# VectorE waits for each GpSimd power before its next two-input instruction, under re-searched engine orders

## The chip, the cores and the metric

The kernel runs on one core of a Trainium2 chip. The metric is the device time of one execution in microseconds (us); the figure for a kernel is the median of several runs. A core has five engines that work side by side, each through its own queue in order: TensorE (matrix products, PE in the profile), VectorE (DVE), ScalarE (ACT), GpSimd (POOL) and SyncE (SP, which here only issues transfers). They wait for one another through semaphores.

## The reference

Two blocks follow each other on a sequence of 2048 rows and 640 columns, in bf16.

```python
def layernorm(x):                        # over the 640 columns, eps 1e-5
    return (x - mean(x)) / sqrt(var(x) + eps)

def A(q, k, v):                          # a gated long convolution
    k_shift = sum(k shifted down by t rows * shift_k[:, t] for t in range(4))
    kv = k_shift * v
    y = irfft(rfft(pad(kv)) * rfft(pad(ssm_k)))[:2048]   # causal, along the rows
    return q * (y + kv * ssm_D)

h = x + A(layernorm(x), A_k, A_v)        # x is A_q
g = silu(layernorm(h) @ w_gate)          # 640 -> 1728
u = layernorm(h) @ w_up
out = h + (g * u) @ w_down               # 1728 -> 640
```

## The kernel before

The 2048 rows are cut into four blocks of 512 (j = 0 to 3), and the columns of the convolution into two halves of 320 (c = 0, 1). For each block and half the kernel works in stages:

- VectorE forms kv: four products of shifted rows of k with the taps, added up, times v. In blocks 2 and 3 two of the additions are made by accumulating transfers that GpSimd issues (line 1089, `kvd`).
- TensorE transforms blocks of kv and of the filter to frequencies with tables (line 694 is the one place where nearly all matmuls are recorded); ScalarE and VectorE copy the results out of PSUM (lines 677, 678, 680, 681). Between two steps of the transform SP's queue shuffles rows by transfers (`sh`, `rs`; line 685). Block 0 uses dense tables and no shuffles.
- VectorE multiplies spectra of pairs of blocks (`m1`, `m2`), adds (`ac`) and combines them (`cr`, `ci`); all these are tensor-by-tensor instructions recorded at line 913.
- TensorE transforms back; VectorE multiplies with the normed q and adds x, which gives h.
- The second layer norm is formed from statistics of h (lines 1003, 1007), h is normed (`hn`), turned (line 1223, or by a transfer for blocks 2 and 3), and the feed-forward runs on it: per block 27 groups of five matmuls with 512 columns, then the product with w_down. ScalarE computes silu (line 1249), VectorE the product of g and u.

The feed-forward of a block is put beside the convolution of later blocks, so that TensorE has work while spectra are formed.

Each layer norm has a short chain of tiny instructions on 2 or 4 columns: VectorE forms variance plus eps (line 1018, `va`; a negated mean at 1045 or 1058), **GpSimd raises it to the power -0.5** (line 1019, `nr`), and VectorE multiplies the negated mean with the result (line 1021, `nm`). The norms themselves (lines 1028 on VectorE, 1029 on ScalarE) use both. There are 12 such powers: one for each block's first norm (4 columns), two for each block's second (2 columns each).

The order on each engine is neither that of the code nor chosen on the chip. All 1640 operations are listed first; a planner (`schedule`) then plays the program through with a duration for each operation and transfer, and at every moment gives a free engine the ready operation with the lowest rank. The ranks are the table `_ORDER`; where an operation could go to ScalarE or VectorE, the table `_WHO` may fix it ("a" or "d"), or the planner chooses. The sequence that comes out is emitted, with semaphores where operations depend on each other; the planner's times themselves are not enforced.

The planner knows that [...] operations of VectorE [...] are marked `lock` (products, combinations, kv, norms, `nm`), and while a power is planned on GpSimd it starts none of them:

```python
if e == "pool" and o.dma is None and c > 0.5 and free["dve"] > t + 1e-9 and dvelock:
    continue
if e == "dve" and o.lock and (poolend > t + 1e-9 or waits):
    continue
```

`deps` of an operation holds the operations that it depends on, with a kind (2: it needs their results); `emit` turns each into a wait.

Of the kernel before, what the change touches and what calls it, by code (L numbers as in the profile page):

```python
# [16 lines left out]
794 795 796 414 566 793 416 567 1244 1246 1235 600 601 1245 198 258 259 857 791 790 401 23 204 24 260 429 785 427 423 199 797 425 433 110 207 421 205  # L17
244 111 0 59 54 71 62 4 19 45 77 69 79 150 101 81 83 93 60 161 163 413 5 120 118 145 82 80 125 50 42 76 91 100 18 20 17 159 151 47 128 555 301 563 147
157 149 1239 10 13 379 377 153 1242 178 181 155 48 1249 102 282 419 43 399 409 11 74 78 44 66 170 84 70 9 206 63 380 146 126 119 117 109 483 99 431 49
248 381 245 190 378 197 270 179 127 67 172 187 995 913 665 660 376 349 672 98 65 893 915 905 890 909 372 675 663 849 272 875 505 865 867 991 979 327  # L20
637 983 336 628 515 647 869 292 559 499 575 855 551 871 985 517 583 316 827 31 507 297 495 287 661 561 981 821 645 716 553 286 466 977 513 873 340 649
639 7 92 1322 158 808 934 710 1001 141 148 90 1090 1410 706 144 75 73 446 448 162 169 171 160 152 108 273 89 34 33 30 36 256 544 949 1314 27 744 736
189 180 107 186 432 177 116 464 291 538 540 748 477 407 405 411 403 221 266 156 154 579 463 535 418 757 1347 533 233 1455 428 1437 484 398 40 953 277
531 246 406 400 243 404 420 470 537 467 306 276 1296 1308 1286 442 482 452 756 438 1011 1274 424 402 412 479 557 581 835 829 195 386 545 541 473 1226
542 532 997 255 168 536 222 462 465 534 478 441 475 408 268 1217 451 1304 711 907 367 530 685 422 426 731 430 1069 1071 345 802 1029 951 1003 232 410
55 15 1221 1447 1433 1445 552 554 779 769 1359 1431 1349 504 497 6 25 383 550 715 443 453 1209 730 471 279 543 219 275 1414 578 1021 695 690 705 961
1223 1065 1048 1031 1063 696 191 1298 959 686 1023 134 56 37 700 72 88 1212 142 95 139 86 390 96 138 801 1200 1105 691 539 112 113 165 1067 1049 1045
1204 137 1230 94 1284 1232 889 184 132 185 183 87 135 46 106 701 1203 1425 188 1372 1192 122 175 176 807 1061 803 1324 58 57 1222 1316 1092 1408 1406
1107 1601 1109 1117 1326 1346 958 1318 1348 1089 1412 1093 1416 1420 721 1418 391 1201 1208 1184 726 32 741 1144 1369 105 1073 1046 1427 1435 1214
1218 1227 35 1177 236 1160 238 254 1589 1302 749 1104 1598 573 1199 385 447 281 449 384 1439 1429 39 38 241 265 1210 237 1597 1635 1152 1590 299 1593  # L30
735 274 681 1594 933 1231 677 395 51 1075 725 1573 1550 1565 1553 1557 1566 1009 1282 936 358 1280 1276 917 1007 1005 396 1577 1019 1017 525 1278 911
892 1581 1582 523 167 53 166 174 524 164 196 1225 1344 1375 264 1549 1631 740 290 1025 417 247 445 218 227 1569 262 1632 1633 1606 1605 1604 1619 1637
1586 415 919 720 240 999 1574 1558 250 269 267 1636 450 1626 1617 1288 501 440 789 472 1 1027 363 480 234 476 474 1585 444 788 1120 1126 194 1030 220
41 782 784 1376 1143 1561 1554 1442 932 935 308 1127 253 242 488 457 239 772 754 547 607 520 1334 257 1111 783 508 588 436 437 261 510 511 577 589 289
16 251 263 252 298 435 792 548 1616 284 1623 1129 68 1329 560 556 834 439 956 210 212 209 203 202 1492 1190 762 1335 1135 1125 1113 64 8 519 136 828
1356 1095 1423 1094 224 910 493 460 973 1510 817 455 387 487 486 459 456 458 1252 974 21 213 352 781 434 1255 1154 635 26 344 115 397 229 114 522 1494
1336 1328 343 226 1331 1436 1333 1136 461 812 481 1262 1467 1464 1147 1198 201 528 1119 215 1610 490 836 454 571 492 1176 658 216 235 231 230 217 225
278 1123 1599 1466 1450 1465 498 502 586 516 514 131 1629 813 1193 503 1026 1366 1350 738 967 1517 1536 1518 1525 1503 133 61 1013 1630 489 491 603
1578 1562 1628 1627 1471 1139 1620 1167 1175 1156 1453 644 833 831 1506 1150 1050 1271 670 1166 1502 1012 249 839 512 1474 1378 1470 1480 1488 966 280
562 1591 1462 1365 359 1155 1486 1535 1402 1399 1370 1128 1137 1377 1482 1243 1367 1342 494 1362 1368 1361 1615 1614 1195 1461 1456 1237 1512 1514  # L40
1138 1267 1454 1478 1339 814 1258 1256 1380 569 633 1458 1490 1392 1178 1430 1452 837 1241 1261 818 1388 939 938 856 1238 228 1179 1130 758 285 496
1300 140 529 124 208 970 1294 1545 1608 776 1338 1440 780 1358 1432 1352 1360 1131 1354 1141 1263 1140 1533 816 392 143 1162 283 1142 763 1133 1132
1310 1424 994 564 1463 565 634 393 1153 895 500 587 103 786 1260 806 1158 805 859 1014 931 1270 388 1428 1364 1363 733 1311 1583 1403 810 394 97 1043
632 1247 368 85 1382 1215 1422 568 1253 1404 708 52 1250 1248 558 271 1259 1174 468 469 546 22 1371 1374 993 12 549 1609 858 767 753 1499 1236 3 838
1257 1341 1254 1373 1146 1186 1438 1426 771 14 1080 1460 787 1390 214 485 1306 1309 1612 1216 1234 1475 745 350 930 940 2 1596 1103 1530 798 799 927
945 900 929 928 104 1290 1240 1015 1625 894 1264 1496 570 925 923 28 1613 1383 1497 1495 1493 1543 1624 1618 593 303 1041 1042 1522 1484 1052 992 1038
1516 313 1476 1587 1559 1602 293 1546 29 323 580 173 572 318 692 625 1555 357 619 627 123 590 1018 947 1016 1024 950 960 1151 304 687 602 830 1417 819
1110 1570 954 1086 1639 1051 952 1057 1055 1054 902 683 1397 1084 804 682 1079 1039 924 922 920 926 121 832 1020 962 1028 1022 679 182 712 693 826
1498 295 1085 506 702 314 1393 1622 707 1081 1082 1066 1058 732 1078 697 1272 1500 722 576 574 1056 1087 1621 1207 1059 1077 678 618 636 1547 1391 509
518 822 1441 809 703 1444 1097 646 868 1033 1528 1224 1443 1485 1389 1487 389 1459 1229 717 1379 1548 1537 1538 288 305 1053 1037 1035 582 584 689 294  # L50
1083 300 1407 713 1508 684 611 1386 1384 727 846 840 1098 1076 1451 1449 597 1387 1072 1062 1068 1064 1515 638 1187 1477 1394 1395 1396 904 347 596
815 626 309 1096 614 1161 594 880 610 604 1595 820 1398 737 310 1099 612 914 1197 874 1060 1044 1047 1457 864 872 862 860 521 606 616 1145 842 1483
1544 863 851 1564 1196 1381 1580 1191 1163 1385 1468 608 1171 824 1202 1206 1600 1603 1002 1275 1074 1233 1285 1542 1185 1194 1446 1448 1183 1088 1526
1159 1323 1507 848 1532 1529 980 976 688 629 854 324 1114 1115 320 642 328 972 338 968 643 319 694 192 1070 718 774 1415 1405 850 1520 315 723 1579
1551 698 704 699 728 982 870 852 1409 1101 1102 1489 1000 330 988 325 876 333 329 648 844 334 984 365 714 709 659 1172 891 371 1189 811 374 1091 1220
916 742 1330 1540 1472 1531 1534 1504 1479 1188 1413 1469 335 948 729 527 1315 1006 193 1148 1501 664 990 375 978 986 866 346 1434 955 348 1411 906
366 339 719 1419 1401 1513 1511 965 724 651 1320 1481 1523 129 1297 957 1307 1295 1353 1305 674 662 963 1283 1008 1321 1112 364 623 969 1180 1400 1168
1277 734 1181 130 1169 620 1303 1281 353 307 1313 739 1173 1273 1010 996 1004 1279 888 908 912 373 918 370 369 743 342 1287 1157 1164 337 1134 599 595
825 847 609 598 311 617 1165 317 1289 1291 1251 1106 605 1116 773 641 650 881 1491 351 585 764 360 211 1521 1355 1345 1228 355 765 1108 296 1219 613
302 1205 853 761 1301 1124 1149 361 897 901 899 884 640 878 971 666 671 800 680 747 746 998 362 841 654 341 657 655 631 332 331 630 668 652 526 223  # L60
653 987 989 382 200 1319 321 1121 751 676 843 322 861 326 312 1213 1040 941 1118 1036 1034 1332 1357 356 1122 964 1268 946 1269 1032 845 624 944 823
615 937 1343 621 622 592 1312 943 354 760 1299 1293 766 942 755 750 877 1327 1317 1325 759 1340 770 1351 752 1337 778 777 1421 591 1292 1100 667 768
# [44 lines left out]
class Prog:  # L107
# [147 lines left out]
    def schedule(self, bias):  # L255
# [10 lines left out]
        t = 0.0  # L266
        left = len(self.ops)
        while left:
            done_any = True
            while done_any:  # L270
                done_any = False
                for e in ("pe", "dve", "act", "sp", "pool"):
# [60 lines left out]
                    if e == "dve":  # L333
                        dvelock = o.lock
# [1055 lines left out]
```

## Time and profile before

| | us |
|---|---|
| median of 7 runs | 297.61 |
| lowest and highest | 296.79, 300.62 |
| profiled execution, its own time | 297.77 |
| its span, first to last instruction | 296.0 |
| TensorE busy | 282.2 (95%) |
| VectorE busy | 235.7 (80%) |
| ScalarE busy | 200.3 (68%) |
| GpSimd busy | 33.1 (11%) |
| the 12 powers (line 1019) together | 19.2 |

A row of the profile's second part has one digit for each fortieth of the span: the busy share in tenths. The chain of waits follows the execution back from its last instruction: at each step to what released it, or to the instruction before it on its engine. A timeline line gives the start, the duration, the engine and line, what is written and read with its shape and count, and in brackets the idle time before it and what ended that. Where several instructions are merged, the duration runs from the start of the first to the end of the last. A line of the waits gives who waited for whom, the total, the number of times and the longest.

### The profile page before, as it was taken

How to read it: one execution, taken by the hardware profiler on the slowest of the kernel's cores; microseconds unless marked ns; L12 is line 12 of the kernel's file. 1: busy time of each engine (PE TensorE's matmuls, PEld its weight loads, DVE VectorE, ACT ScalarE, POOL GpSimd, SP SyncE). 2: the span in 40 equal slices, each digit the busy share in tenths (PEclk: the TensorE clock that was granted, in tenths of full speed). 3: DMA queues.
4: the chain of work that ended last, by engine and by line, in shares of the span. 5: the costliest groups of instructions: out<-in, count | busy, mean ns of one | idle time of the engine just before them, and what ended most of it. 6: DMA issues, size and time to landing. Idle time of an engine off the chain costs nothing.

```text
span 296.0 us, 5206 instructions
## 1 busy us (share of the span) xinstructions
PE 282.2 (95%) x1820; PEld 153.7 (52%) x1820; DVE 235.7 (80%) x479; ACT 200.3 (68%) x484; POOL 33.1 (11%) x31
## 2 busy tenths in 40 slices
PE   7898979799999899999999999999999999999996
PEld 1465645444444356664445467654444676444574
DVE  3999899998999889999999999992899753214422
ACT  3388889999888878777899895778995221242000
POOL 2000500208111121101100313100020020000000
DMA  6999999835685788728802037754001143000001
GB/s 185 331 368 377 300 359 308 269 121 125 168 179 145 179 200 212 222 67 202 222 33 103 1 91 204 176 132 180 24 0 44 47 90 89 2 0 0 2 22 66
DMA packets 44051, 43.25 MB, mean 146 GB/s; under 512 B 14895, under 2 KB 38889, under 8 KB 43898
## 3 DMA queue, kind: packets, MB, share of 16 engines
q1 hardware_dynamic: 39640, 38.30, 41.6%
q0 software_dynamic: 3328, 3.97, 8.3%
q10 hardware_dynamic: 1058, 0.66, 0.7%
q8 instruction: 14, 0.23, 0.4%
q14 instruction: 11, 0.09, 0.1%
HBM read 20.63 MB, written 2.62 MB: 79 GB/s over the span
## 4 chain that ended last, share of the span: by engine, by line
PE 70%; DVE 12%; ACT 8%; DMA 4%; POOL 3%; issue 2%; ACTq 0%; DVEq 0%; SPq 0%
PE ps L694 69%; DVE sb L913 10%; ACT sb L677 5%; DMA sb<-sb 4%; POOL stt L1019 3%; ACT sb L1029 1%; ACT sb L680 1%; PE ps L823 1%; DVE sb L678 0%; DVE sb L1028 0%; PE ps L1223 0%; DVE sb L779 0%; DVE sb L681 0%; ACT sb L1049 0%; DVE stt L1003 0%
## 5 line engine op out<-in xcount | busy, mean ns | idle before, releaser
L694 PE MATMUL ps<-sb 128*128 128x320 bf16 (+1 forms) x1220 | 227.6, 340 | 6.1 <-DVE sb L913 2.0
L913 DVE TENSOR_TENSOR sb<-sb 128x1280 bf16<-128x1280 bf16 (+3 forms) x286 | 171.1, 658 | 4.2 <-ACT sb L677 3.5
L694 PEld LDWEIGHTS ps<-sb 128*128 128x128 bf16 (+1 forms) x1220 | 116.6, 99 | 100.1 <-issue 7.9
L677 ACT ACTIVATE sb<-ps 128x320 bf16<-128x320 f32 (+2 forms) x282 | 111.4, 483 | 26.2 <-PE ps L694 21.3
L694 PE MATMUL ps<-sb,tab 128*64 128x320 bf16 (+2 forms) x512 | 63.3, 302 | 3.6 <-DMA sb<-sb 2.5
L913 DVE TENSOR_TENSOR sb<-ps,sb 128x512 bf16<-128x512 f32 (+2 forms) x46 | 28.0, 617 | 44.7 <-PE ps L694 38.4
L1249 ACT ACTIVATE sb<-ps 128x512 bf16<-128x512 f32 (+1 forms) x56 | 33.8, 606 | 33.0 <-PE ps L694 32.5
L694 PEld LDWEIGHTS ps<-sb,tab 128*64 128x64 f16 (+2 forms) x512 | 31.6, 101 | 35.7 <-issue 13.3
L1019 POOL TENSOR_TENSOR stt<-stt 128x2 f32<-128x2 f32 (+1 forms) x12 | 19.2, 1601 | 134.6 <-DVE stt L1018 94.8
L1029 ACT ACTIVATE sb<-sb,stt 128x320 bf16<-128x320 bf16 (+1 forms) x31 | 22.3, 750 | 7.0 <-DVE stt L1021 6.6
L680 ACT ACTIVATE sb<-ps 128x320 bf16<-128x320 f32 x49 | 18.5, 447 | 5.1 <-PE ps L694 4.8
L1089 POOL DMA_DIRECT2D sb<-sb x12 | 12.4, 1031 | 68.4 <-DVE sb L913 34.0
L678 DVE CAST sb<-ps 128x320 bf16<-128x320 f32 x26 | 12.0, 481 | 3.4 <-PE ps L694 3.4
L1003 DVE BATCH_NORM_STATS2 stt<-sb 128x6 f32<-128x320 bf16 x32 | 14.4, 477 | 0.0
L1049 ACT ACTIVATE sb<-sb,stt 128x640 bf16<-128x640 bf16 x16 | 13.5, 842 | 0.7 <-DVE stt L1045 0.6
L1042 ACT ACTIVATE sb<-sb 128x640 bf16<-128x640 bf16 x16 | 11.9, 742 | 0.6 <-DMA sb<-in_A_q_dram 0.5
L1028 DVE TENSOR_SCALAR sb<-sb,stt 128x320 bf16<-128x320 bf16 (+1 forms) x17 | 6.2, 383 | 0.7 <-DMA sb<-sb 0.7
L823 PE MATMUL ps<-sb 128*128 128x128 bf16 (+1 forms) x48 | 3.9, 231 | 0.4 <-ACT sb L677 0.3
L823 PEld LDWEIGHTS ps<-sb 128*128 128x128 bf16 (+1 forms) x48 | 3.2, 119 | 1.7 <-issue 1.4
L1223 PE MATMUL ps<-sb 128*128 128x128 bf16 x40 | 3.1, 219 | 0.9 <-ACT sb L677 0.9
L1021 DVE TENSOR_TENSOR stt<-stt 128x2 f32<-128x2 f32 (+1 forms) x12 | 1.8, 146 | 2.4 <-POOL stt L1019 2.4
L681 DVE TENSOR_SCALAR sb<-ps 128x320 bf16<-128x320 f32 x7 | 3.3, 480 | 0.4 <-PE ps L694 0.4
(24 smaller groups left out, 24.3 us busy)
## 6 DMA issues: line engine op xcount, KB each, us to landing
sb<-sb SPq DMA_DIRECT2D x72, 160.0 KB, 2.2
sb<-sb POOLq DMA_DIRECT2D x12, 320.0 KB, 4.2
out_dram<-sb SPq DMA_DIRECT2D x16, 160.0 KB, 2.0
sb<-in_A_k_dram SPq DMA_DIRECT2D x8, 280.0 KB, 3.4
sb<-in_B_w_down_dram SPq DMA_DIRECT2D x13, 160.0 KB, 6.6
sb<-cst_den SPq DMA_DIRECT2D x8, 256.0 KB, 7.4
sb<-in_A_v_dram SPq DMA_DIRECT2D x6, 320.0 KB, 5.3
sb<-in_A_q_dram SPq DMA_DIRECT2D x6, 320.0 KB, 4.6
```

What stands on the lines that cost most here:

```text
L677: fns = {"act": lambda a: a.activation(out=dst(), in_=src(), func=ACTF.Copy), "dve": lambda v: v.tensor_copy(out=dst(), in_=src())}
L678: "dve": lambda v: v.tensor_copy(out=dst(), in_=src())}
L680: fns = {"act": lambda a: a.activation(out=dst(), in_=src(), func=ACTF.Copy, scale=scale), "dve": lambda v: v.tensor_scalar(out=dst(), in0 ...
L694: return lambda t: t.matmul(o(), l(), r(), start=st, stop=sp)
L913: return lambda v: v.tensor_tensor(out=o(), in0=a(), in1=b_(), op=op)
L1003: vec(dve1(CW, False), lambda v: v.bn_stats(st6(l, j, b, c), V(xt, b * D + c * CW, CW)), [(xt, (b, c))], [(ST, ("s", l, j, b, c))], prio, ...
L1019: P.op({"pool": 0.75}, lambda g: g.tensor_tensor(out=y, in0=va, in1=stt[:, 420:420 + hi - lo], op=ALU.pow), c1 + [(ST, "half")], c3, prio, ...
L1029: "act": lambda a: a.activation(out=dst(), in_=src(), func=ACTF.Identity, scale=rs(l, j, b), bias=tmv(l, j, 3)[:, b:b + 1])},
L1042: P.op({"act": act_c(D) + 0.22}, lambda a, b=b, jt=jt: a.activation(out=V(jt, 0, D), in_=V(xt, b * D, D), func=ACTF.Copy, accum_out=tmv(l, ...
L1049: P.op({"act": act_c(D) + 0.3}, lambda a, b=b, jt=jt: a.activation(out=V(jt, 0, D), in_=V(xt, b * D, D), func=ACTF.Square, bias=tmv(l, j, ...
L1089: P.op({"pool": 1.35}, [lambda g: g.dma_start(v4(t0), src(), accum_op=ALU.add)], [(t0, 0)] + cells, [(t0, 0)], prio, dma=(2.1, 2.1, 0.8), ...
L1249: P.op({"act": act_c(n)}, lambda a: a.activation(out=dst(), in_=src(), func=ACTF.Silu), rd, wr, -1000, name=f"si{nm}", after=after)
```

## The change

`schedule` remembers the last power that it has placed on GpSimd. When it next places an operation on VectorE that is marked `lock`, it adds the power to that operation's dependencies, so that `emit` puts a wait for the power ahead of it; then it forgets the power. This is done once for each power, for the first such operation in VectorE's sequence.

The two tables are replaced: all ranks of `_ORDER`, and `_WHO`, where 174 operations in place of 182 are fixed to ScalarE and 58 in place of 52 to VectorE. The search that made the new ranks varied the delays of transfers only. The operations themselves, their number, shapes and buffers stay as they are.

```diff
 _ORDER = """
-794 795 796 414 566 793 416 567 1244 1246 1235 600 601 1245 198 258 259 857 791 790 401 23 204 24 260 429 785 427 423 199 797 425 433 110 207 421 205
...
+797 857 856 794 795 414 1236 1237 547 417 839 566 500 601 569 416 836 567 796 790 791 81 83 20 270 276 467 545 495 297 1142 1444 1443 18 827 1508 1245
...
@@ def schedule(self, bias):
-        pemode, dvelock, poolend = 0, False, 0.0
+        pemode, dvelock, poolend, last = 0, False, 0.0, None
...
                     if e == "dve":
                         dvelock = o.lock
+                        if o.lock and last is not None:
+                            o.deps[last] = 2
+                            last = None
                     if e == "pool" and o.dma is None and o.engs[e] > 0.5:
-                        poolend = t + o.engs[e]
+                        poolend, last = t + o.engs[e], o
```

## The prediction

> **What bounds the kernel now.** I read the page's 40 slices first, then its chain of waits, then the timelines of VectorE and GpSimd around each power.
>
> ```profile
> PE   7898979799999899999999999999999999999996
> DVE  3999899998999889999999999992899753214422
> POOL 2000500208111121101100313100020020000000
> ```
>
> A slice is 7.4 us. TensorE looks busy everywhere, but a busy TensorE need not be at its peak, so I counted its matmuls by form in stretches. Late in the kernel (250 to 270 us) 48 matmuls of 512 columns fill 10 us: 0.208 us each, 0.407 ns per column. At that rate (forms on half the array run in pairs, so they count half) the 97,200 columns of 0 to 60 us are worth 39.6 us: 20.4 us lost. From 60 to 80 us only 1.3 us is lost, from 80 to 110 us 4.6 us, from 110 to 230 us some 0.6 us in ten, and then almost nothing up to 280. So TensorE sets the end from 60 us on, and time can be won in two places: ahead of 60 us, where VectorE and ScalarE feed it (from 20 to 60 us VectorE is idle for 1.7 us of 40, ScalarE for 2.9), and between 80 and 110 us. The chain says the same, with GpSimd on it:
>
> ```profile
> PE 70%; DVE 12%; ACT 8%; DMA 4%; POOL 3%; issue 2%; ACTq 0%; DVEq 0%; SPq 0%
> L1019 POOL TENSOR_TENSOR stt<-stt 128x2 f32<-128x2 f32 (+1 forms) x12 | 19.2, 1601 | 134.6 <-DVE stt L1018 94.8
> ```
>
> L1019 is the power (the reciprocal root of a layer norm), 12 times; 3% of the span is two of them, 3.73 us at 30.7 and 5.20 us at 66.9. Now GpSimd's timeline, and VectorE's beside it:
>
> ```profile
> 30.73 3.72 POOL L1019 TENSOR_TENSOR stt<-stt 128x4 f32<-128x4 f32 x1 [26.34 <-DVE stt L1018]
> 53.45 0.70 POOL L1019 TENSOR_TENSOR stt<-stt 128x2 f32<-128x2 f32 x1 [19.00 <-DVE stt L1058]
> 66.89 5.19 POOL L1019 TENSOR_TENSOR stt<-stt 128x4 f32<-128x4 f32 x1 [11.24 <-DVE stt L1018]
> ```
>
> ```profile
> 30.56 2.99 DVE L913 TENSOR_TENSOR sb<-sb 128x640 bf16<-128x640 bf16 x6
> 34.49 0.16 DVE L1021 TENSOR_TENSOR stt<-stt 128x4 f32<-128x4 f32 x1 [0.94 <-POOL stt L1019]
> ...
> 53.35 0.88 DVE L1003 BATCH_NORM_STATS2 stt<-sb 128x6 f32<-128x320 bf16 x2
> ...
> 66.72 4.50 DVE L913 TENSOR_TENSOR sb<-sb 128x512 bf16<-128x512 bf16 x7
> 72.11 0.16 DVE L1021 TENSOR_TENSOR stt<-stt 128x4 f32<-128x4 f32 x1 [0.90 <-POOL stt L1019]
> ```
>
> The reader is to see that the power at 30.73 ends 0.90 us after the last of six products (30.56 + 2.99 = 33.55; 34.45), the one at 66.89 ends 0.86 us after the last of seven (71.22; 72.08), and that VectorE then stands idle for it anyway. The one at 53.45, beside statistics with a single input, took 0.70. A power alone costs 0.7 to 0.9 us; the rest of a long one is waiting behind products. Five are long (3.72, 5.19, 1.20, 2.27, 1.52): 9.9 us over 0.8 each.
>
> [...] Of a wait on GpSimd the trace has its own number: 0.03 to 0.04 us from a power's end to the start of L1021. [...]
>
> **The change part by part.** It adds a wait: in the planner's order, the first instruction of VectorE marked `lock` after a power depends on that power. Where that instruction is L1021 itself the wait is there already. The planner kept such instructions out of a power's 0.75 us before too, but nothing held the engine to it. No instruction is added or removed; all ranks are new, and of the places by hand ScalarE has 174 for 182, VectorE 58 for 52.
>
> *The wait at 30.7 us.* The power ends by about 31.6 instead of 34.45, and L1021 comes 2.8 us earlier. The six products that stood ahead now stand behind it, about 0.9 us later; the 0.94 us of idling after them goes, so VectorE loses nothing net. ScalarE's norms (L1029, from 34.88) can start up to 2.8 us earlier. But VectorE and ScalarE are all but full here, so most of this is one piece of work before another. What I can point to is TensorE's 1.27 us of idling at 39.67, put down to L1029. Bounds: 0 and 2.8 us of gain; I take 0.9.
>
> *The wait at 66.9 us.* L1021 comes 4.3 us earlier, the seven products 0.9 us later, idle again exchanged (0.90). GpSimd's next instruction, the issue of an accumulating transfer at 72.04, comes earlier as well. TensorE is at 94% of its late rate up to 80 us (filled by the feed-forward), so nothing is won at once. On the chain this power leads through L1028 and ScalarE to a shuffle at 77.40 and to TensorE at 81.87. What may be won is the loss between 80 and 110 us above the usual 0.6 in ten: 4.6 - 1.8 = 2.8 us, of which these waits are part:
>
> ```profile
> 81.87 0.84 PE L694 MATMUL ps<-sb,tab 128*64 128x320 bf16 x8 [0.39 <-DMA sb<-sb]
> 103.97 1.79 PE L694 MATMUL ps<-sb,tab 128*128 128x320 bf16 x12 [1.85 <-DMA sb<-sb]
> ```
>
> The second waits for a shuffle of a later stage, which the new order may or may not start sooner. Bounds 0 and 2.8 us; I take 1.0, about a third.
>
> *The other ten.* Seven took 0.69 to 0.89 and had no one in their way: nothing. The three at 110.77, 163.63 and 215.63 lose 0.4 + 1.5 + 0.7 us; their L1021 didn't wait, and TensorE runs at 92 to 95% of its late rate there: no gain. Each wait can cost VectorE up to 0.9 us, 2.7 in all. Cover: feed-forward matmuls on TensorE, and VectorE's own idle time after 200 us (6.8 us in 200 to 220). I take nothing; without the cover it costs those 2.7.
>
> *The new order.* The 72 shuffles on SP's queue, the 16 smaller ones that spread filter rows, its loads, and the 12 accumulating transfers of GpSimd (1.03 us to issue, 4.2 to land) can move past each other. The profile of before can't show where. Bound it by what transfers cost TensorE directly now, 2.5 us in three waits: 2.5 won if all go, 2.5 lost if as many come. The six more places on VectorE are at most 6 × 0.48 = 2.9 us of it, off ScalarE at 0.46 each. I take nothing and keep ±2.5 for the range.
>
> Sum: 0.9 + 1.0 = 1.9 us. The profiled execution took 297.77 us, 1.77 of it around its span of 296.0; the median of the seven runs is 297.61. So the span falls to about 294.1, and the median to **295.7 us**.
>
> **The rivals.**
> - *Both delays return in full.* 2.8 + 2.8 = 5.6 us, so 292.0. For it: both powers are on the chain. Against: VectorE is idle for only 1.7 us between 20 and 60 us, 0.9 of which is exchanged.
> - *Hidden anyway.* Before 60 us work fills VectorE and ScalarE whatever its sequence; after it TensorE is full. Then the time stays at 297.6. The table of busy engines speaks for this; the 1.27 and 1.85 us of idling TensorE against.
> - *Slower: VectorE stands for a power that is late itself.* GpSimd takes its queue in order, and its accumulating transfers wait for one another there:
>
> ```profile
> POOL sb L1089 <- DMA sb<-sb: 11.2, 3, 4.1
> ```
>
> Three waits, the longest 4.1 us. A power that comes behind such an issue is late by up to 4.1 + 0.9 for the issue; before, VectorE ran on with products, now all its instructions behind the first product stand, with them the inverse transforms on TensorE and the ScalarE copies after them. Price 4.1 + 0.9 = 5.0 us a time. VectorE is idle for 6.3 us in all between 10 and 200 us, so one such stall with the 2.7 us above is more than it can take back (7.7 over 6.3), and at the front nothing covers it. One stall uncovered, less the 1.9 won: 300.7 us. Against: five powers (109.9 to 186.1 us) stand between accumulating transfers now, and each was released by VectorE, none by a transfer. A new order that hardware follows worse ends on this side too.
> - *The change doesn't do what it says*: if the search has put L1021 or single-input work after each power, the added waits are empty and the new order alone acts. A short power then still shows that the order did it; the gain is the same.
>
> **How the numbers follow.** A measurement here tells about 0.5% (1.5 us) from no change: 296.1 and 299.1. The forecast, partial return (294.0 to 296.5), gets 0.38, of which 0.02 lies within 0.5%; full return 0.13; hidden 0.19; slower 0.30, large because an order that wins on paper has no profile yet. Faster 0.36 + 0.13 = 0.49, same 0.02 + 0.19 = 0.21, slower 0.30. Range 292.8 to 300.7: it leaves out half of full return and some four tenths of the slower cases. The likeliest case alone: 294.0 to 296.5.
>
> **What would show it.** Right: no power over 1.0 us (L1019 about 9.5 us in all for 19.2); POOL at 1% or less on the chain; waits of L913 or another product for L1019, under 1 us each; first feed-forward matmul ahead of 60.6 us; fewer than 4.6 us lost from 80 to 110 us. Wrong: a wait for L1019 of several us on VectorE; powers short but feed-forward no earlier (hidden); TensorE idle after 110 us.

## The result, and the profile after

The change made the kernel slower: 301.44 us median of 12 runs (299.56 to 303.78) against 297.92 for the kernel before in the same comparison; the ratio is 1.0112, with a 95% interval of 1.0083 to 1.0142. A second comparison gave 1.0100 (1.0072 to 1.0129). The forecast was 295.7, the range ended at 300.7. Medians are of all executions; ratios and their intervals leave out a few slower ones (over 1.5% above the fastest), so the two need not agree to the last digit.

The profiled execution took 299.56 us, the shortest of its twelve, with a span of 297.8. All lines of the code stand three further down: the power is L1022, the product with its result L1024, VectorE's tensor-by-tensor instructions L916, the matmuls L697. From the page of the changed kernel, the busy tenths in 40 slices and the row of the powers:

```profile
PE   6798989799989999999999999999999999999996
DVE  3889999998999899999999999982899852313322
POOL 2000100204111122101100214000030010000000
...
L1022 POOL TENSOR_TENSOR stt<-stt 128x2 f32<-128x2 f32 (+1 forms) x12 | 14.8, 1234 | 141.2 <-DVE stt L1021 99.3
```

The powers take 14.8 us in place of 19.2. Its timelines of GpSimd and VectorE at the two powers that were long:

```profile
31.92 1.21 POOL L1022 TENSOR_TENSOR stt<-stt 128x4 f32<-128x4 f32 x1 [27.38 <-DVE stt L1021]
67.61 2.25 POOL L1022 TENSOR_TENSOR stt<-stt 128x4 f32<-128x4 f32 x1 [10.71 <-DVE stt L1021]
```

```profile
31.74 1.22 DVE L916 TENSOR_TENSOR sb<-sb 128x640 bf16<-128x640 bf16 x2
33.16 1.63 DVE L916 TENSOR_TENSOR sb<-sb 128x640 bf16<-128x640 bf16 x3 [0.20 <-POOL stt L1022]
34.71 0.16 DVE L1024 TENSOR_TENSOR stt<-stt 128x4 f32<-128x4 f32 x1
...
67.43 1.56 DVE L916 TENSOR_TENSOR sb<-sb 128x1280 bf16<-128x1280 bf16 x2
69.89 4.51 DVE L916 TENSOR_TENSOR sb<-sb 128x1280 bf16<-128x1280 bf16 x8 [0.90 <-POOL stt L1022]
74.31 0.16 DVE L1024 TENSOR_TENSOR stt<-stt 128x4 f32<-128x4 f32 x1
```

The power of 5.19 us has become one of 2.25: two products that stand ahead of the wait still hold it up (they end at 68.99 us, the power at 69.86), and then the 0.9 us follow in which VectorE stands (the bracket of the second L916 line). But L1024, which uses the result, starts at 34.71 and 74.31 us, where L1021 started at 34.49 and 72.11 before. The power is done after a shorter time and its result is used later. Part of that is the new order: the instruction that feeds the first power (L1021 here, L1018 before) itself starts at 31.67 us for 30.49, and at the second power ten products stand ahead of L1024 in place of seven. VectorE's waits for a power, from its table of waits (who for whom, total, times, longest):

```profile
DVE sb L916 <- POOL stt L1022: 2.9, 5, 0.9
DVE sb L1031 <- POOL stt L1022: 0.8, 1, 0.8
```

That is 3.7 us of standing still; before it was 2.4, all at the product with the result (then L1021). The chain of waits of this profile can be followed back only to 222.9 us, so it says nothing on the part ahead. There I compared the start of the same operation in both traces. TensorE's timeline of the first microseconds of the change, then of the kernel before:

```profile
2.78 6.15 PE L697 MATMUL ps<-sb 128*128 128x512 bf16 x16 [2.78 <-DVE sb L731]
8.86 1.37 PE L826 MATMUL ps<-sb 128*128 128x128 bf16 x12
11.84 1.51 PE L697 MATMUL ps<-sb 128*128 128x320 bf16 x5 [1.61 <-DVE sb L681]
```

```profile
1.71 1.89 PE L694 MATMUL ps<-sb 128*128 128x512 bf16 x4 [1.71 <-DVE sb L728]
3.84 4.33 PE L694 MATMUL ps<-sb 1*128 1x320 bf16 x12 [0.25 <-DVE sb L711]
8.22 1.35 PE L823 MATMUL ps<-sb 128*128 128x128 bf16 x12
10.37 2.85 PE L694 MATMUL ps<-sb 128*128 128x320 bf16 x10 [0.80 <-ACT sb L677]
```

The first matmul waits for a memset of zeros, which the new order has put fourth on VectorE (second before). The first dense matmul, which begins TensorE's steady work, comes at 11.84 for 10.37 us; ahead of it stand 1.61 us of waiting for copies that the new order gave to VectorE, while ScalarE was idle:

```profile
13.12 0.44 ACT L680 ACTIVATE sb<-ps 128x320 bf16<-128x320 f32 x1 [5.58 <-PE ps L697]
```

So there were two suspects: the added waits, and the new order, above all its first 12 us. Where the text below says L1021, it means the product with the result, as the kernel before numbers it; in views of versions with added lines it is L1024 or L1025.

### The profile page after: what moved, and what is told of

The parts are those of the page before. It is cut to its first block, busy times and chain, and to the rows that moved or that the text cites. A ratio compares the mean times of both kernels' runs of the same rounds, so it can differ in the third digit from the quotient of the medians.

```text
span 297.8 us, 5215 instructions
## 1 busy us (share of the span) xinstructions
PE 283.2 (95%) x1820; PEld 152.9 (51%) x1820; DVE 237.6 (80%) x484; ACT 198.6 (67%) x479; POOL 28.5 (10%) x31
## 5 line engine op out<-in xcount | busy, mean ns | idle before, releaser
L697 PE MATMUL ps<-sb 128*128 128x320 bf16 (+1 forms) x1220 | 228.6, 341 | 7.6 <-DVE sb L731 2.8
L916 DVE TENSOR_TENSOR sb<-sb 128x1280 bf16<-128x1280 bf16 (+3 forms) x286 | 170.9, 661 | 5.9 <-POOL stt L1022 2.9
L697 PEld LDWEIGHTS ps<-sb 128*128 128x128 bf16 (+1 forms) x1220 | 116.3, 99 | 102.0 <-issue 11.1
L697 PE MATMUL ps<-sb,tab 128*64 128x320 bf16 (+2 forms) x512 | 64.7, 303 | 3.4 <-DMA sb<-sb 1.3
L916 DVE TENSOR_TENSOR sb<-ps,sb 128x512 bf16<-128x512 f32 (+2 forms) x46 | 28.1, 617 | 43.2 <-PE ps L697 31.2
L697 PEld LDWEIGHTS ps<-sb,tab 128*64 128x64 f16 (+2 forms) x512 | 31.3, 101 | 36.8 <-issue 12.6
L1022 POOL TENSOR_TENSOR stt<-stt 128x2 f32<-128x2 f32 (+1 forms) x12 | 14.8, 1234 | 141.2 <-DVE stt L1021 99.3
L683 ACT ACTIVATE sb<-ps 128x320 bf16<-128x320 f32 x45 | 17.3, 457 | 3.5 <-PE ps L697 3.0
L681 DVE CAST sb<-ps 128x320 bf16<-128x320 f32 x28 | 12.9, 484 | 5.1 <-PE ps L697 4.8
L684 DVE TENSOR_SCALAR sb<-ps 128x320 bf16<-128x320 f32 x11 | 5.2, 485 | 1.0 <-PE ps L697 1.0
L1045 ACT ACTIVATION_READ_ACCUMULATOR sb<-sb 128x1 f32 x16 | 3.3, 209 | 0.0
```

What stands on the lines that cost most here:

```text
L681: "dve": lambda v: v.tensor_copy(out=dst(), in_=src())}
L683: fns = {"act": lambda a: a.activation(out=dst(), in_=src(), func=ACTF.Copy, scale=scale), "dve": lambda v: v.tensor_scalar(out=dst(), in0 ...
L697: return lambda t: t.matmul(o(), l(), r(), start=st, stop=sp)
L916: return lambda v: v.tensor_tensor(out=o(), in0=a(), in1=b_(), op=op)
L1022: P.op({"pool": 0.75}, lambda g: g.tensor_tensor(out=y, in0=va, in1=stt[:, 420:420 + hi - lo], op=ALU.pow), c1 + [(ST, "half")], c3, prio, ...
L1045: P.op({"act": act_c(D) + 0.22}, lambda a, b=b, jt=jt: a.activation(out=V(jt, 0, D), in_=V(xt, b * D, D), func=ACTF.Copy, accum_out=tmv(l, ...
```

## The experiments

The theories: (1) the order lost the time and the waits do what the prediction says; (2) the waits lost it; later, (3) the waits move idle time but can't bring L1021 forward (the theory of place). All ratios are to the kernel before, run on the same chip; each version has 6 to 22 executions, and 1% is 3 us.

**The two parts apart, and the front repaired.** Each of the first two keeps the sequence of all engines as it was, since the dependency is added when an operation's place is already chosen; the traces show the same instructions in the same order on every engine.

new_order_no_wait is the change less these lines, old_order_wait the kernel before with them:

```diff
                         if e == "dve":
                             dvelock = o.lock
+                            if o.lock and last is not None:
+                                o.deps[last] = 2
+                                last = None
```

> The new ranks and places, the same sequence on every engine, but VectorE gets no added wait for a power. If the loss of 3.5 us lies in the new order (theory 1), this stays at 301 to 303 us: as slow as the change or a little slower, with powers of 3 us and more. If it lies in the waits (theory 2), this is near the kernel before, 297 to 298.5 us.

Measured: 298.87 us, ratio 1.0062 (1.0037 to 1.0087).

> The ranks of before, the same sequence on every engine, with the waits for the powers added. Theory 1 (the order lost, the waits do what the prediction's steps say): 295.7 to 297.5 us, no power above 2.3 us. Theory 2 (the waits lost): 300 to 302 us. Hidden anyway: 297.9 within 0.5%.

Measured: 298.90 us, ratio 1.0041 (1.0020 to 1.0061). Neither theory alone held: the order costs about 1.8 us, the waits about 1.2 on either order (1.0100 and 1.0112 against 1.0062; 1.0041 against 1). Together that is about the loss. And the wait on the old order is the plainest test of the prediction's sum, because nothing else differs. Its timelines of VectorE and GpSimd at the first power (lines as in the change):

```profile
30.54 1.24 DVE L916 TENSOR_TENSOR sb<-sb 128x640 bf16<-128x640 bf16 x2
32.71 1.86 DVE L916 TENSOR_TENSOR sb<-sb 128x640 bf16<-128x640 bf16 x4 [0.94 <-POOL stt L1022]
34.49 0.16 DVE L1024 TENSOR_TENSOR stt<-stt 128x4 f32<-128x4 f32 x1
```

```profile
30.73 1.95 POOL L1022 TENSOR_TENSOR stt<-stt 128x4 f32<-128x4 f32 x1 [26.34 <-DVE stt L1021]
```

The power is 1.95 us long for 3.72, and L1024 starts at 34.49 us, to the hundredth where it started before. The 0.94 us of idling stand ahead of four of the products now, not behind all six. That is theory 3: VectorE takes its queue in order, and the product with the result stands behind the six products there, even when the power ends early.

new_order_front: the change, with the first 12 us laid out much as before. The edit moves operations in the finished sequences: three memsets to the head of VectorE's, and two tap copies and one copy of the turned filter to ScalarE's, ahead of its first dense copy.

```diff
         P.schedule(0.8)
+        V0, A0 = P.order["dve"], P.order["act"]
+        named = lambda q, n: [o for o in q if o.name == n]
+        for n in ("one", "onz", "wwz"):
+            o = named(V0, n)[0]
+            V0.remove(o)
+            V0.insert(0, o)
+        for n in ("tap1", "tap0", "kte00"):
+            o = named(V0, n)[-1 if n == "tap1" else 0]
+            V0.remove(o)
+            o.eng = "act"
+            A0.insert(next(k for k, p in enumerate(A0) if p.name[:2] == "de"), o)
...
```

> The change, with the first 12 us laid out as before: the memset that feeds the first matmuls comes first on VectorE, and two tap copies and one copy of the turned filter go from VectorE to idle ScalarE. If 1.2 to 1.6 us of the loss arise there (TensorE's steady work begins at 11.84 us for 10.37, and its pace doubles at 16.7 for 15.0), this is 299.7 to 300.3 us and the first dense matmul comes at 10.6 us or earlier. If the front is made up for later, it stays at 301.4.

Measured: 298.85 us, ratio 1.0051 (1.0032 to 1.0070), against 1.0100 to 1.0112 unrepaired: about 1.6 us won. The first dense matmul came at 9.28 us.

change_again: the change once more.

> The change as it is, for a comparison on the same chip: 301.4 us, and a second profile, since the first one (299.56 us) was the fastest of its runs. Where the time of an ordinary execution goes should show against the first: theory 1 expects TensorE's pace to double later in it than at 16.7 us, or transfers to land later.

Measured: 300.16 us; its profile is of an execution of 301.75. Against the first profile it lost 0.74 us between 32 and 36 us, and 1.0 between 55 and 63. The first step is the first power: it took 1.94 us for 1.21, and VectorE stood 0.94 us for it instead of 0.20. The second step stands in the page's row of the clock that TensorE was granted, where one slice dips:

```profile
PEclk9999999899999999999999999999999999999999
```

The granted clock was 0.50 from 58 to 61 us, 0.98 in the 4 us before and 0.97 in the 4 us behind, which makes about 3.4 us at half the clock, from 57.8 us on. TensorE is busy for 2.70 of the 4 us from 54 to 58; in the first profile it is busy for 2.48 of them and the clock stays at 1.00, so what brought the fall isn't shown. The pace doubled at 16.9 us, as in the first profile (there the first starts 0.136 us apart, for 0.267 before, are those at 16.79 and 16.93), so that part of the expectation failed.

**Which waits cost, and what place is worth.**

wait_two_early is old_order_wait with the wait for the powers at 30.7 and 66.9 us alone; wait_late_only has the names of eight others there (`nr11`, `nr02`, `nr12`, `nr03`, `nr13`). The two of block 0's second norm (`nr10`) need no mark, since the first marked instruction behind them is L1021 itself.

```diff
-                                o.deps[last] = 2
+                                if last.name in ('nr00', 'nr01'):
+                                    o.deps[last] = 2
```

> The order of before, with the added wait for the powers at 30.7 and 66.9 us alone. Theory of place: L1021 stands behind the products in VectorE's own queue, so the wait only moves VectorE's idle time from behind the products to ahead of them; L1021 starts at 34.5 and 72.1 to 72.5 us as before, and the time is that of before, within 0.3% (297.0 to 297.9 us on the chip of the last runs). The prediction's step: L1021 2.8 and 4.3 us earlier, 1.9 us won (295.1). The loss of some 1.3 us of the wait on the old order, if it lay in these two: 298.2.

Measured: 297.34 us, ratio 0.9997 (0.9982 to 1.0011). The two waits from which the prediction drew all its gain are worth nothing, and cost nothing. Its profile is of an execution of 301.95 us, which lost its time behind 134 us; up to 73 us it shows where the result is used:

```profile
34.50 0.15 DVE L1025 TENSOR_TENSOR stt<-stt 128x4 f32<-128x4 f32 x1
72.33 0.15 DVE L1025 TENSOR_TENSOR stt<-stt 128x4 f32<-128x4 f32 x1
```

Before it was at 34.49 and 72.11 us. Of the 0.22 us at the second power, 0.14 are there already when the power is fed (66.78 for 66.64).

> The order of before, with the added wait for the ten other powers alone. Theory of place: where L1021 is far behind and nobody waits for the power, the wait is new idle time of VectorE (1.0 us at 163 us, up to 1.0 at 110 us), and TensorE's feed-forward waits for VectorE's product soon after: 0.9 to 1.5 us slower than before, 298.0 to 298.5. If TensorE's queue covers it: as before, 297.0.

Measured: 298.05 us, ratio 1.0017 (1.0003 to 1.0030), about 0.5 us slower. VectorE's timeline at the power of 163 us (lines four further down than before):

```profile
162.86 0.15 DVE L1022 TENSOR_SCALAR stt<-stt 128x4 f32<-128x4 f32 x1
162.93 1.15 DVE L917 TENSOR_TENSOR sb<-sb 128x1280 bf16<-128x1280 bf16 x2
165.08 1.23 DVE L917 TENSOR_TENSOR sb<-sb 128x640 bf16<-128x640 bf16 x3 [1.00 <-POOL stt L1023]
```

Here nobody waited for the power before (its result was used at 171.2 us), so the 1.00 us is new idle time. The loss is smaller than expected, as part of it is covered.

l1021_ahead: the order of before without waits, but L1021 moved.

```diff
         P.schedule(0.8)
+        V0 = P.order["dve"]
+        for n in ("00", "01"):
+            o = next(p for p in V0 if p.name == "nm" + n)
+            V0.remove(o)
+            V0.insert(next(k for k, p in enumerate(V0) if p.name == "va" + n) + 1, o)
...
```

> The order of before without added waits, but in VectorE's queue L1021 of the powers at 30.7 and 66.9 us stands directly behind the instruction that feeds its power, ahead of the products. L1021 then starts near 31.6 and 67.7 us, and no product runs beside the power. If the prediction was wrong only in the place of L1021: 1.9 us faster, 295.1. If the users of the result stand behind other work in their own queues (ScalarE was idle for 0.4 us ahead of its first norm): 296.7 to 297.3, as before.

Measured: 297.71 us, ratio 1.0020 (1.0004 to 1.0035). ScalarE's timeline shows how little even a result 2.7 us earlier brings; first with L1021 at 31.81 us, then before, with it at 34.49:

```profile
33.52 0.98 ACT L677 ACTIVATE sb<-ps 128x320 bf16<-128x320 f32 x2 [0.24 <-PE ps L694]
34.46 1.20 ACT L1029 ACTIVATE sb<-sb,stt 128x320 bf16<-128x320 bf16 x2
```

```profile
33.52 0.98 ACT L677 ACTIVATE sb<-ps 128x320 bf16<-128x320 f32 x2 [0.24 <-PE ps L694]
34.88 1.20 ACT L1029 ACTIVATE sb<-sb,stt 128x320 bf16<-128x320 bf16 x2 [0.38 <-DVE sb L913]
```

The first norm starts 0.42 us earlier, not 2.7, since copies stand ahead of it in ScalarE's own queue. At the second power L1021 comes 3.85 us earlier (68.26 for 72.11), but VectorE's norms, which stand behind the products, come 0.68 us later (73.28 for 72.60). VectorE in turn waited longer at the powers (2.9 us in all for 2.4). Slightly slower is what came out, where the expectation said as before. No run moved the norms forward too, so what an early result is worth to a user that can take it stays open.

TensorE's idling of 1.27 us, from which the prediction argued, is still there. Its line before, in old_order_wait and in l1021_ahead:

```profile
39.67 1.26 PE L694 MATMUL ps<-sb 128*128 128x320 bf16 x8 [1.27 <-ACT sb L1029]
39.67 1.26 PE L697 MATMUL ps<-sb 128*128 128x320 bf16 x8 [1.27 <-DVE sb L916]
39.91 1.26 PE L694 MATMUL ps<-sb 128*128 128x320 bf16 x8 [1.27 <-DVE sb L913]
```

The page puts a wait down to what ended last, and before that was the norm on ScalarE, at 39.65 us, 0.04 us behind a product on VectorE (39.61). In the other two the norm ends at 39.52 and 39.76, the product at 39.61 and 39.85. In all three the matmul starts 0.06 us after the product, so it follows VectorE's product; an earlier norm alone could not move it.

**The front by halves, without the waits.** new_front_no_wait is new_order_front less the added waits; the next two take one half of its repair each; the last repeats it.

> The new order with the repaired first 12 us, without the added waits. If the front is the whole loss of the order and the waits the rest of it, this equals the kernel before within 0.3% (296.5 to 297.6 us). If the new order loses elsewhere too, 298 us or more.

Measured: 297.42 us, ratio 0.9981 (0.9960 to 1.0002). Its VectorE hardly waits for powers at all, though one lasts 5.93 us:

```profile
DVE stt L1021 <- POOL stt L1019: 0.2, 1, 0.2
```

The first power shows why. Its lines here, then in front_memset_only, with the same five products and L1021 behind them:

```profile
29.39 1.21 POOL L1019 TENSOR_TENSOR stt<-stt 128x4 f32<-128x4 f32 x1 [24.63 <-DVE stt L1018]
29.21 2.76 DVE L913 TENSOR_TENSOR sb<-sb 128x640 bf16<-128x640 bf16 x5
31.89 0.15 DVE L1021 TENSOR_TENSOR stt<-stt 128x4 f32<-128x4 f32 x1
...
30.97 3.48 POOL L1019 TENSOR_TENSOR stt<-stt 128x4 f32<-128x4 f32 x1 [26.22 <-DVE stt L1018]
30.79 2.76 DVE L913 TENSOR_TENSOR sb<-sb 128x640 bf16<-128x640 bf16 x5
34.49 0.16 DVE L1021 TENSOR_TENSOR stt<-stt 128x4 f32<-128x4 f32 x1 [0.94 <-POOL stt L1019]
```

In one the power ends at 30.60 us, in the midst of the products, and costs VectorE nothing; in the other it ends behind them, and L1021 comes 0.94 us later. It was short in both profiles of this version and in the first of the change, all three of executions faster than their version's median (296.68, 296.28 and 299.56 us for 297.42, 296.93 and 301.44), and long in the second of the change. So the 0.2 us may be these executions' luck; what decides it is not shown.

> The new order without the added waits, and of the repair of the front only the memset: the zeros that feed the first matmuls come first on VectorE. The first matmul should start 1.5 us earlier (1.3 for 2.8 us). If both halves of the repair add up, this takes about three fifths of the 2.4 us between the new order without waits (1.0062) and the repaired one (0.9981): 1.001 to 1.002. [...]

Measured: 298.39 us, ratio 1.0037 (1.0020 to 1.0055). The expected 1.001 to 1.002 was missed; the ratio lies between those without the repair (1.0062) and with both halves (0.9981).

> The new order without the added waits, and of the repair only the three copies moved from VectorE to ScalarE, which is idle from 7.5 to 13 us in the change. The gap of TensorE ahead of the first dense matmul should shrink from 1.6 to about 1.0 us. If both halves add up: 1.003 to 1.005. If the copies are hidden behind the late first matmul: 1.006.

Measured: 298.77 us, ratio 1.0055 (1.0035 to 1.0075), not told apart from no repair.

> The new order with both halves of the repair and without the added waits, once more: whether it beats the kernel before. 0.998 again if so, which with the first measurement would leave 1 out; 1.000 if the first one was chance.

Measured: 296.93 us, ratio 0.9991 (0.9976 to 1.0006). Both intervals hold 1: this version is as fast as the kernel before, and not shown to be faster.

The start of the first dense matmul orders these versions (new order, no waits):

| repair | first dense matmul, us | ratio |
|---|---|---|
| none | 11.84 | 1.0062 |
| copies | 11.04 | 1.0055 |
| memset | 10.33 | 1.0037 |
| both | 9.5 to 9.6 | 0.9981, 0.9991 |
| (kernel before) | 10.37 | 1 |

So the front is a cause of the order's loss. The table doesn't say through which engine: the same copies also take VectorE's time, and L1018 of the first norm orders the versions alike (31.68, 31.24, 30.72, then 29.14 and 28.94 us; 30.49 before). The front isn't the whole either: with the memset alone the dense matmuls start as early as before, L1021 even at the same 34.49 us, and 1.1 us are still lost. In its profile they are lost behind that point (a span of 297.0 us for 296.0). In the profiles with both halves L1021 comes 2.6 and 2.8 us earlier than before, and the span is only 1.1 and 1.5 us shorter. What loses this is open.

**An early start on the old order.** The same three memsets first, in the kernel before.

> The kernel before, without waits, with three memsets that feed the first matmuls put first on VectorE (zeros for the warm-up, ones for the taps). The first matmul should start at 1.3 for 1.7 us, the first dense matmul at about 9.7 for 10.4, L1018 of the first norm at about 29.9 for 30.5 us. If an early start is worth what it was on the new order (1.3 us earlier there gave 0.4 us less than before), some 0.4 to 0.7 us faster than before: 0.998. If it is lost later: 1.000.

Measured: 296.53 us, ratio 0.9997 (0.9979 to 1.0014), though the first dense matmul came at 9.60 us and L1018 at 29.73. No gain is shown: on the old order an early start isn't worth what the late one cost on the new.

## Why the prediction was wrong, point by point

The forecast's 1.9 us of gain did not come, and two terms that it put at nothing cost about 1.2 (the waits) and 1.8 us (the order).

- **"L1021 comes 2.8 us earlier" (and 4.3) is the step that failed.** The timeline shown in the prediction has the six products ahead of L1021 on VectorE. The prediction says that they "now stand behind it"; but the added wait moves nothing in VectorE's queue, and they stay ahead of it. Before: products, then 0.94 us of rest of the power, then L1021. With the wait: the power, then products, then L1021. The sum is the same, 34.49 us both times. With these two waits alone on the old order the 0.9 + 1.0 us of gain became 0 (0.9997), so the step isn't mis-sized but void. The support for the 0.9, TensorE's 1.27 us put down to L1029, was a misreading too: that matmul follows a product of VectorE.
- **"Idle again exchanged" was right**, and is the whole effect of those two waits. VectorE's idle time at powers, each from one profile, is a rough index of what the waits did:

| | VectorE idle for powers, us | ratio |
|---|---|---|
| before | 2.4 | 1 |
| old order, two early waits | 2.5 | 0.9997 |
| old order, late waits | 3.4 | 1.0017 |
| old order, all waits | 3.5 | 1.0041 |
| new order, no waits | 1.1 | 1.0062 |
| the change | 3.7 | 1.0100, 1.0112 |
| new order, front repaired, no waits | 0.2 | 0.9981, 0.9991 |
| the same with waits | 3.7 | 1.0051 |

  Within one order, more idle time goes with more time: 1.1 us more cost about 1.2 (old, all waits), 2.6 more 1.1 to 1.5, 3.5 more some 1.9. On the new order a wait can even bring the result later: at the second power L1021 starts 6.21 us behind L1018 without waits, and the same pair in the change is 6.95 us apart, because without the wait the power is over by the time that the ten products are. Late and early waits by themselves add up to 0.1%, all together measured 0.4% (0.2 to 0.6); with the intervals of the parts the sum reaches 0.3%, so a difference isn't shown.
- **"The other ten ... I take nothing; without the cover it costs those 2.7."** The cover was missing in part, and the late waits cost 0.5 us on the old order.
- **"The new order ... I take nothing and keep ±2.5."** It cost 1.8 us, inside that bound. But the bound was made from transfers, and what the runs showed is a memset and three copies in the first 12 us; what transfers had in it wasn't measured. The prediction didn't look at the start of TensorE, though the page gives its first slice 7 tenths and, counted again at its own rate, about 10 of the 20.4 us that it calls lost ahead of 60 us lie ahead of 20. (That its forms on half the array run in pairs shows in the trace of before: at 81.87 us eight of them take 0.84 us, where at 39.67 us eight on the whole array, with as many columns, take 1.26.)
- **The slower rival** had the right sign and a mechanism that the trace doesn't show: no power came late behind an accumulating transfer (all twelve were released by VectorE); VectorE's waits at powers were 0.9 us at most in the change, never 5. VectorE did stand for powers, but for powers that were on time. Its price (300.7) came close by accident.
- **What would show it**: powers of at most 1.0 us, 9.5 in all, were expected as a sign of success. Shorter ones came (14.8 us for 19.2), but up to 2.25 us each, since two products still stand ahead of a wait, and they went with a slower kernel. For the two early waits "hidden anyway" (0.19) is what came: the table of busy engines, which the prediction set aside for 1.27 us of TensorE idling, was the better guide.

## What to carry to other kernels

A long instruction on the chain is worth shortening only if its user can run sooner: look where the user stands in its own engine's queue, and what stands ahead of it (here a power went from 3.72 to 1.95 us, and its user started at 34.49 us both times). A wait added to an engine's queue can move that engine's idle time (0.94 us at that power) or add to it (1.00 us at the one of 163 us); here it didn't bring the product with the result forward. A wait that the page puts down to one engine may have had a second one 0.04 us behind: compare a trace in which only one of the two moved. When a whole order is replaced, read the first microseconds of each engine too: here their repair won 1.6 us with the waits and over 2 us without.

## What the runs showed that I had not expected

- A power that took 5.93 us beside VectorE's products cost VectorE no more than 0.2 us (new order, front repaired): L1021 came up in its queue at 70.89 us, 0.04 us after the power ended.
- TensorE's matmuls of 320 columns started 0.267 us apart up to 15.0 us in the profile before and up to 16.7 us in that of the change, then 0.136 us apart. In the change matmuls had filled most of 2.8 to 10 us; what sets the moment isn't shown. (In new_order_front the first sixteen, of 512 columns, took 5.72 us for 6.15.) In two profiles of the new order (new_order_no_wait and change_again) the granted clock fell to half for about 3.4 us near 57.8 us, at a cost of 1.0 us in the one compared, and in one of the old order (wait_two_early) at 145.7 us. The fall doesn't explain the 1.1 us that stay open in the new order. The mean granted clock of the three profiled executions with one fall is 0.993 or 0.994. Without one (0.999 or 1.000) four executions of front_memset_only have a median of 298.32 us and 21 of the kernel before, on the same chip, one of 297.12: 1.2 us apart. The kernel before has such a mean too, in the other 8 of its 29 executions there, which took 0.8 us longer.
